# Two attention and two gated-unit layers on one core: tiles three and four as a pair, a shared tail in the output projection, and a last down projection in 288-column pieces

## The chip, the cores and the metric

The kernel runs on one core of a Trainium2 chip. The metric is the device time in microseconds of one execution; lower is better. PE is the matmul engine (TensorE), DVE the vector engine, ACT the scalar engine, POOL is GpSimd, and SP issues the DMAs. All times are in us unless ns is written.

## The reference

The input is 2048 rows of 576 numbers. Four layers follow each other, each with a residual addition: attention, gated unit, attention, gated unit, with the same weights in both rounds.

```python
def _A_ref(x, wqkv, wo):          # H = 32 heads of 18, W = 8 positions, dilation 2
    qkv = (lambda x, *d: x.transpose(*d))((x @ wqkv).reshape(B, S, 3, H, Dh), 2, 0, 3, 1, 4)
...
    idx = pos[:, None] - off[None, :]          # off = 0, 2, ..., 14
    logits = einsum("bhsd,bhswd->bhsw", q, kg) * scale
    attn = softmax(where(mask, logits, -1e9))
    o = einsum("bhsw,bhswd->bhsd", attn, vg)
    return o.reshape(B, S, D) @ wo
def _B_ref(x, w_gate, w_up, w_down):           # F = 4608
    return ((x @ w_gate) * (x @ w_up)) @ w_down
x = x + _A_ref(_layernorm(x), ...)
x = x + _B_ref(_layernorm(x), ...)
x = x + _A_ref(_layernorm(x), ...)
x = x + _B_ref(_layernorm(x), ...)
```

A position attends to itself and the seven positions 2, 4, ..., 14 before it, so an attention tile needs only 14 rows (the halo) of the tile ahead of it.

## The kernel before

**Tiles and items.** The 2048 rows are 16 tiles of 128. They are worked on in items: an item is one tile (`nst` = 1) or a pair of tiles (`nst` = 2) in one attention layer and the gated unit behind it. `seq` (L1042 to L1049) lists them: for the first eight tiles, layer pair 0 and then layer pair 1; then the same for the last eight. The first four tiles are single items in layer pair 0, everything else is in pairs, so there are 18 items, numbered `j` from 0. All weights but w_down stay in SBUF. w_down is read again for each item, in 18 loads of 288 KB (L840 to L848) into seven buffers.

**An item's attention** (`attention`, L493). `head` (L406) makes the layer norm of the tile's rows and their transpose: statistics on DVE (L414, L415), the root on ACT (L429, L430), a small DVE step (L433), the normalised rows on ACT (L439), and the transpose. For `j` < 5 the transpose is made on PE (six instructions, L452 and L454) through the single PSUM bank `pa` and copied out by ACT (L457); later items use a DMA transpose (L445). Then come the QKV projection (`project`, L517; matmuls L527; evacuation by ACT and DVE), the scores on DVE (products L676 or L697, sums L680 to L685), the sum over each head on PE (L691), the softmax on DVE and ACT (L717 to L733), the spread of the weights over the heads' partitions (on PE and ACT, L742 and L748, for `j` < 5; by DMA through DRAM otherwise, L752 and L755), the weighted sum of v on DVE (L772, L786) into `oT`, the output projection on PE (L805 for pairs, L826 for single tiles), the residual addition on DVE (L796), and a second `head`, whose result `xnT_B` feeds the gated unit.

**Half arrays.** For pairs, most matmuls read only 64 of the array's 128 rows. `both` (L464) alternates those on the lower and on the upper 64 rows, which write different PSUM banks, so that two run side by side. Each accumulation is made in two passes, `first` and not; between them a one-element ACT copy (`fence`, L469, L471) keeps the passes apart. Single tiles use the full array (L876, L928), except for the last 64 of the 576 contracted rows (L887).

**The output projection of a pair** (L797 to L819). `oT` has 576 numbers a row in five groups: four of 128 and a last one, `t` = 4, of 64, which stands in partitions 0 to 63. `strip(i, r, hh, first)` lists the matmuls of tile `i`, array half `r` and column half `hh`. The lower half has five of them, the upper four, in each of the four strips, since the last group is only in the lower partitions.

**The gated unit** (`glu`, L853). 36 blocks of 128 columns of gate and up. A pair takes units of two blocks (`quarter`, L894), a single tile units of four blocks in groups of three units (`full`, `tails`, L871 to L892). `evac` (L907): ACT copies the gate (L911), DVE multiplies (L912). The down projection follows in three phases (`down`, L919, for single tiles; `down2`, L957, for pairs), each followed by additions to the residual on DVE (L939, L941 or L948). The pair's down projection writes 512 columns into one PSUM bank and 64 into another. The very last one of the kernel is written out in an order of its own (L991 to L999) on the full array: eight blocks of the second tile, all twelve of the first, the last four of the second; each tile is then added (512 and 64 columns) and stored with one DMA of 144 KB.

**What sets the order.** Nothing is issued directly. Each step is recorded with `op(engine, cost, function, reads, writes, ...)`, and `Plan.run` (L84) lists them: it keeps a clock for each engine from the costs written in the code, and takes again and again the step that can start first, with ranks and margins (`rank`, `prio`, `margin`) that decide between items. The functions are then called in that order, and each engine runs its instructions strictly in it. PSUM banks are handed out by the same plan: `unit` (pairs of banks), `pa` (one bank) and `boot`. At `j` == 4 (L1070) the banks `pa` and `acct` join the units. While PE has nothing to do before the first gated unit, the plan fills it with idle matmuls (L1077).

`xtmp` (L300) is room inside the residual buffer `xf` in which the rows of the fifth and sixth tile are loaded early, so that the fifth item's `head` can run ahead; `guard` (L792) keeps the item that writes there behind its readers. `place` (L484) says which q, k, v buffers an item uses.

Of the kernel before, what the change touches and what calls it, by code (L numbers as in the profile page):

```python
# [169 lines left out]
def kernel(  # L170
# [78 lines left out]
    wd = [sb(f"wd{i}", [P, 2, D]) for i in range(NWD)]  # L249

# [80 lines left out]
    def setup_b():  # L331
        def mk_zero():
            for t_ in qT_:
                nc.gpsimd.memset(t_[TL:P, KF, :], 0.0)
            for t_ in kv_:
                nc.gpsimd.memset(t_[TL:P, :, KF, :], 0.0)
            nc.gpsimd.memset(q_x[TL:P, KF, :], 0.0)
            nc.gpsimd.memset(kv_x[TL:P, :, KF, :], 0.0)
            for t_ in halo:
                nc.gpsimd.memset(t_[:], 0.0)  # L340
            nc.gpsimd.memset(wo_p[TL:P, KF, :], 0.0)
        op("POOL", 2600, mk_zero, w=[f"{x}{t}{i}" for x in "qkv" for t in (4, "H") for i in ZN] + [f"halo{i}" for i in range(n_al)] + ["wo_z"])
# [61 lines left out]
    wok = ["wo_z", "wot0", "wot1"] + [f"wo{dd}" for dd in range(4)]  # L404

    def head(src, keys, nst, dst, key, prio, ab, on_pe, mg, c0=0, halves=False):  # L406
# [3 lines left out]
        for i in range(nst):  # L410
            def stats(i=i):
                xr = src(i).rearrange("p (a b) -> p a b", a=2)
                for a in range(2):
                    nc.vector.bn_stats(out=st[:, ia + i, a, :], in_=xr[:, a, :])  # L414
                nc.vector.bn_aggr(out=mv[:, ia + i, :], in_=st[:, ia + i])  # L415
# [7 lines left out]
            op("DVE", 970, stats, r=[keys[i]], w=[f"mv{ab}{ia + i}", f"st{ab}{ia + i}0", f"st{ab}{ia + i}1"], prio=prio)  # L423
# [4 lines left out]
        def rs():  # L428
# [3 lines left out]
        op("ACT", 440, rs, r=mk + ["eps"], w=rk, prio=prio)  # L432
        op("DVE", 75, lambda: nc.vector.scalar_tensor_tensor(nmr[:, sl], mv[:, sl, 0], -1.0, rstd[:, sl], op0=ALU.mult, op1=ALU.mult),  # L433
           r=mk + rk, w=nk, prio=prio)
        for i in range(nst):
# [6 lines left out]
            op("ACT", 770 if on_pe else 1100, apply, r=[keys[i], nk[i], rk[i]], w=[f"xn{ab}{ia + i}"], prio=prio)  # L442
# [41 lines left out]
    def place(j, nst):  # L484
        if nst == 1:
            z, h = j // 2, j % 2
            return [2 * z + h], qT_[z][:, :, h * P:h * P + P], kv_[z][:, :, :, h * (HALO + P):(h + 1) * (HALO + P)], h * P
        if j == 4:
            return ["x"], q_x, kv_x, 0
        z = (j + 1) % 2  # L490
        return [2 * z, 2 * z + 1], qT_[z][:], kv_[z][:, :, :, 0:HALO + CH], 0

    def attention(j, la, t0, nst):  # L493
# [3 lines left out]
        on_pe = j < 5  # L497
        prio, mg = (1, 0) if fast else (3, 500 if j < 6 else 1200)
# [7 lines left out]
        if j != 4:  # L506
            head(lambda i: xin[:, i0 + i, :], xin_k, nst, xnT_A, "xA", prio, 0, on_pe, mg, c0)
# [9 lines left out]
        def project(tag, au, bu, tl, ea, eb, dkeys):  # L517
# [32 lines left out]
            if nst == 2:  # L550
                o = None
                fs = {ka: {}, kb: {}}
                for first in (True, False):
                    for u, key, parts in ((ua, ka, au), (ub, kb, bu)):
                        r0, r1 = (0, 1) if first else (1, 0)
                        kw = dict(pair=(ua, ub), margin=400) if o is None else dict(after=o, need=u)
# [30 lines left out]
            else:  # L587
# [11 lines left out]
                o1 = pieces(ua, au, ka, True, False, late["wo"] if 2 <= j < 4 else None, margin=400, pair=(ua, ub))  # L599
# [44 lines left out]
        else:  # L644
# [89 lines left out]
        op("DVE", 86 + 2.05 * n, soft3, r=["Lt", "zs"], w=["s13"], prio=prio - 1)  # L734
        if on_pe:
# [56 lines left out]
        guard = {3: ["xt0", "xt1"], 5: zk_x}.get(j, [])  # L792
# [4 lines left out]
        if nst == 2:  # L797
# [4 lines left out]
            def strip(i, r, hh, first):  # L802
                def one(t):
                    rows = slice(TL * r, TL * r + TL)
                    return nc.tensor.matmul(bank(hh, us[i])[:, 0:HD], lhsT=oT[rows, t, i * P:(i + 1) * P], rhs=wo_p[rows, t, hh * HD:(hh + 1) * HD],  # L805
                                     start=(first and t == 0), stop=(not first and t >= KF - 1), skip_group_check=True)
                return [lambda t=t: one(t) for t in range(KF + 1 - r)]
            for first in (True, False):
                for i in range(nst):
                    kw = dict(pair=tuple(us), margin=mg) if o is None else dict(after=o, need=us[i])  # L810
                    o = op("PE", KT * TILE * HD, lambda i=i, first=first: both(strip(i, 0, 0 if first else 1, first), strip(i, 1, 1 if first else 0, first),
                                                                                           None if first else fs[i]),
                           r=["oT", "oTt", *wok], w=[f"wo{j}_{i}"], prio=0, half=True, **kw)
                    if first:
                        fence(fs[i], lambda i=i: bank(0, us[i])[0:1, 0:1], [f"wo{j}_{i}"])
# [17 lines left out]
        head(lambda i: xs_f[:, i0 + i, :], fk, nst, xnT_B[j % NXB], f"xB{j % NXB}_", prio - 1, 1, on_pe, mg, halves=fast)  # L833
# [19 lines left out]
    def glu(j, t0, nst, last):  # L853
# [103 lines left out]
        def down2(ph, hsl, half):  # L957
# [33 lines left out]
            todo = {0: spans(ph), 1: spans(ph)}  # L991
            lead = spans(ph)[:8]
            order = [(1, x) for x in lead] + [(0, x) for x in spans(ph)] + [(1, x) for x in spans(ph)[8:]]
            for x, (i, (m, e, ft)) in enumerate(order):
                kw = dict(pair=(use, tl)) if x == 0 else {}
                bb("PE", 122, lambda i=i, m=m, e=e, ft=ft: [f() for f in two(i, slice(0, P), m, e, ft, ft == n0, ft == n1)],
                   r=[f"h{hsl[m]}", f"wd{wb(ft)}"], w=[f"acc{j}_{ph}{i}"], **kw)
                if ft == n1:
                    settle2(i, use, tl, True, f"acc{j}_{ph}{i}")  # L999

        units = {}
        for ph in range(nph):
# [37 lines left out]
            settle(ph, use)  # L1040

    seq = []  # L1042
# [12 lines left out]
    load_x(2, 1)  # L1055
    load_x(3, 1)
# [6 lines left out]
    for j, (l, t0, nst) in enumerate(seq):  # L1063
        if l == 0 and j >= 4:
            load_x(t0, nst)
# [4 lines left out]
        if j == 4:  # L1070
# [40 lines left out]
```

## Time and profile before

| | us |
|---|---|
| median of 3 runs | 1057.23 (1056.66 to 1058.14) |
| the profiled execution | 1056.22 |
| its span in the profile | 1054.4 |
| granted TensorE clock in it | 0.998 |

The span runs from the first to the last instruction of the profiled execution; 1.8 us of that execution lie outside it. In the profile's rows of groups stand the line, the engine, the operation, what is written and read, the shapes, the count, then the busy time in us and the mean duration of one in ns, and after the second bar the idle time of the engine ahead of them. In the timeline's rows stand the start, the duration, the engine, the line and the same names. Matmuls overlap: their price is the step from one start to the next, not the duration.

### The profile page before, as it was taken

The page shows a single profiled execution, that of the slowest core. Times are in us where ns is not written, and L with a number is a line of the kernel's source. Part 1 is how long each engine was busy: PE and PEld are TensorE (multiplying, and loading weights), DVE is VectorE, ACT ScalarE, POOL GpSimd, SP SyncE. Part 2 cuts the span into 40 slices and gives each one's busy share as a digit, 9 for nine tenths or more (in the row PEclk, how much of TensorE's full clock was granted, in tenths as well). Part 3 has the DMA queues.
Part 4 walks back from the last instruction along what each step waited for, and adds up shares of the span by engine and source line. Part 5 has one row for each costly group of instructions (what it writes and reads, how often), then busy time and mean ns, then how long its engine had stood idle before and what let it go on. Part 6 is the DMA issues. An engine that isn't in the chain of part 4 may idle for free.

```text
span 1054.4 us, 39972 instructions
## 1 busy us (share of the span) xinstructions
PE 1040.7 (99%) x17845; PEld 829.9 (79%) x17863; DVE 786.2 (75%) x1477; ACT 410.8 (39%) x1090; POOL 8.9 (1%) x33
## 2 busy tenths in 40 slices
PE   7999999999999999999999999999999999999998
PEld 4888878787788898778887777877887788777776
DVE  7688989786979996979798876676878758833332
ACT  6752254343334544333434323334344252232221
POOL 3000000000000000000000000000000000000000
PEclk9999999999999999999999999999999999999999
DMA  9966563524262543254444534334353334343332
GB/s 272 317 186 194 177 185 104 155 63 145 69 149 81 146 105 107 70 149 128 120 93 107 140 114 118 93 115 95 93 151 82 99 90 126 116 135 96 116 101 69
DMA packets 146828, 133.68 MB, mean 127 GB/s; under 512 B 42272, under 2 KB 146016, under 8 KB 146656
## 3 DMA queue, kind: packets, MB, share of 16 engines
q1 hardware_dynamic: 146656, 131.13, 44.1%
q8 instruction: 139, 2.28, 0.9%
q14 instruction: 33, 0.27, 0.1%
HBM read 118.51 MB, written 4.06 MB: 116 GB/s over the span
## 4 chain that ended last, share of the span: by engine, by line
PE 82%; DVE 11%; DMA 4%; SPq 1%; issue 1%; ACT 1%; DVEq 0%; ACTq 0%
PE pg L900 15%; PE pu L900 14%; PE pu L968 9%; PE pg L968 8%; PE pa L900 5%; PE acct L900 5%; PE pg L527 4%; PE pu L527 3%; PE pu L876 3%; PE pg L876 3%; PE pg L928 2%; DVE scr L772 2%; DVE oT L786 2%; DMA scr<-a_dram 2%; DVE h L912 2%; PE pg L805 1%
## 5 line engine op out<-in xcount | busy, mean ns | idle before, releaser
L900 PE MATMUL pg<-xnT_B,wg 64*128 64x256 bf16 x3072 | 395.3, 269 | 0.5 <-DVE xf L796 0.5
L900 PE MATMUL pu<-xnT_B,wu 64*128 64x256 bf16 x3072 | 395.0, 269 | 0.5
L900 PEld LDWEIGHTS <-wg 64*128 64x128 bf16 x4032 | 367.7, 94 | 29.7 <-issue 2.6
L900 PEld LDWEIGHTS <-wu 64*128 64x128 bf16 x4032 | 366.8, 94 | 23.5 <-issue 0.6
L968 PE MATMUL pg<-wd,h 64*128 64x512 bf16 (+1 forms) x972 | 252.0, 377 | 0.8 <-DVE h L912 0.8
L968 PE MATMUL pu<-wd,h 64*128 64x512 bf16 (+1 forms) x971 | 252.1, 377 | 0.0
L912 DVE TENSOR_TENSOR h<-pu,g_sb 128x512 bf16<-128x512 f32 x228 | 153.5, 686 | 73.8 <-ACT g_sb L911 69.7
L968 PEld LDWEIGHTS <-h 64*128 64x128 bf16 (+1 forms) x1992 | 115.1, 94 | 100.3 <-DVE h L912 2.9
L911 ACT CAST g_sb<-pg 128x512 bf16<-128x512 f32 x228 | 132.1, 586 | 127.6 <-PE pg L900 91.6
L471 ACT COPY tok<-pu 1x1 f32<-1x1 f32 x254 | 37.4, 147 | 258.7 <-PE pu L900 191.8
L900 PE MATMUL acct<-xnT_B,wg 64*128 64x256 bf16 x960 | 130.7, 269 | 0.0
L900 PE MATMUL pa<-xnT_B,wu 64*128 64x256 bf16 x960 | 130.6, 269 | 0.0
L969 PEld LDWEIGHTS <-h 64*128 64x128 bf16 (+1 forms) x1992 | 114.1, 95 | 1.3 <-issue 0.6
L527 PEld LDWEIGHTS <-wqkv 64*128 64x128 bf16 (+1 forms) x2044 | 103.2, 94 | 15.0 <-issue 2.6
L900 PE MATMUL pg<-xnT_B,wgu_t 64*128 64x256 bf16 x384 | 103.3, 269 | 0.0
L900 PE MATMUL pu<-xnT_B,wgu_t 64*128 64x256 bf16 x384 | 103.3, 269 | 0.0
L969 PE MATMUL pa<-wd,h 64*128 64x64 bf16 (+1 forms) x540 | 102.1, 189 | 0.1
L969 PE MATMUL acct<-wd,h 64*128 64x64 bf16 (+1 forms) x540 | 102.1, 189 | 0.0
L697 DVE TENSOR_TENSOR scr<-qT,kv 128x1280 bf16<-128x1280 bf16 x104 | 82.4, 816 | 25.9 <-ACT kv L611 25.9
L786 DVE TENSOR_TENSOR oT<-oT,scr 128x1280 bf16<-128x1280 bf16 (+1 forms) x119 | 90.9, 764 | 3.2
L527 PE MATMUL pg<-xnT_A,wqkv 64*128 64x256 bf16 (+2 forms) x826 | 92.6, 260 | 0.5 <-ACT wqkv L355 0.3
L527 PE MATMUL pu<-xnT_A,wqkv 64*128 64x256 bf16 (+2 forms) x786 | 90.1, 262 | 0.8 <-DVE kv L609 0.4
(156 smaller groups left out, 1598.2 us busy)
## 6 DMA issues: line engine op xcount, KB each, us to landing
wd<-in_B_w_down_dram SPq DMA_DIRECT2D x324, 288.0 KB, 4.4
scr<-a_dram SPq DMA_DIRECT2D x52, 128.0 KB, 2.7
wg<-in_B_w_gate_dram SPq DMA_DIRECT2D x6, 768.0 KB, 10.0
wu<-in_B_w_up_dram SPq DMA_DIRECT2D x6, 768.0 KB, 11.3
out_dram<-xf SPq DMA_DIRECT2D x16, 144.0 KB, 3.0
xb<-in_A_x_dram SPq DMA_DIRECT2D x6, 288.0 KB, 2.9
a_dram<-scr SPq DMA_DIRECT2D x13, 128.0 KB, 2.4
scr<-in_A_wqkv_dram SPq DMA_DIRECT2D x4, 288.0 KB, 3.6
```

The source lines that it names most:

```text
L471: box["at"] = nc.scalar.copy(tok[0:1, :], src())
L527: return nc.tensor.matmul(bank(p_, u)[0:m, e * n:(e + 1) * n], lhsT=wqkv[r_, k, w0:w0 + m], rhs=xnT_A[r_, k, c0:c0 + n], start=start, stop ...
L697: op("DVE", 70 + 2.6 * n, lambda p_=p_, e=e: nc.vector.tensor_tensor(late["prod"][p_ % 2][:, e, :, 0:n], qT[:, :, 0:n], kT[:, :, HALO - DI ...
L772: nc.vector.tensor_tensor(js(dst), js(vT[:, :, o0:o0 + n]), abw, op=ALU.mult)
L786: op("DVE", 70 + 2.63 * n, lambda i_=i_: nc.vector.tensor_tensor(oT[:, :, 0:n], oT[:, :, 0:n], late["prod"][i_ % 2][:, 0, :, 0:n], op=ALU. ...
L876: nc.tensor.matmul(pt[:, e * n:(e + 1) * n], lhsT=w_[:, k, ft * P:(ft + 1) * P], rhs=xT[:, k, 0:n], start=(first and k == 0 and e == 0), s ...
L900: return nc.tensor.matmul(ps[:, e * n:(e + 1) * n], lhsT=w_, rhs=xT[rows, k, 0:n], start=(first and e == 0 and k == 0), stop=(not first an ...
L911: op("ACT", 490, lambda: nc.scalar.copy(g_sb[gs][:, 0:ul], pg[use["slot"]][:, 0:ul]), r=[f"wg_{j}_{u}"], w=[f"g{gs}"], prio=0, due=True)
L912: op("DVE", 605, lambda: nc.vector.tensor_tensor(hb[hs][:, 0:ul], pu[use["slot"]][:, 0:ul], g_sb[gs][:, 0:ul], op=ALU.mult), r=[f"wu_{j}_{ ...
L928: nc.tensor.matmul((pg, pu)[i][use["slot"]][:], lhsT=lhs, rhs=wt[:, e % 2, 0:512], start=first, stop=fin)
L968: return [lambda: nc.tensor.matmul((pg, pu)[i][use["slot"]][:], lhsT=lhs, rhs=wt[rows, e % 2, 0:512], start=first, stop=fin, skip_group_ch ...
L969: lambda: nc.tensor.matmul((pg, pu)[i][tl["slot"]][:, 0:TL], lhsT=lhs, rhs=wt[rows, e % 2, 512:D], start=first, stop=fin, skip_group_check ...
```

## The change

- `seq`: only the first two tiles are single items; tiles three and four become one pair, the third item (`j` = 2). There are 17 items, and every later item's number falls by one. `on_pe` (transposes and spread on PE) now holds for `j` < 3, `pa` and `acct` join the units at `j` == 2, and the numbers in `place`, `guard` and the margins move with it. The rows of the fifth item (the seventh and eighth tile) also go through `xtmp`: its `head` is cut in two (`parts`), the normalisation being recorded at `j` == 2 behind the softmax and the transpose, by DMA, at `j` == 3. The second `head` of `j` == 2 gets a higher priority, a smaller margin and its statistics in halves.
- Output projection: the last 64 rows of wo are loaded into both partition halves, and ACT copies the second tile's last group of `oT` to partitions 64 to 127. The first tile's last matmul runs on the lower half of the array and the second tile's on the upper.
- The very last down projection: each tile's 576 columns in two pieces of 288, each with its own bank, addition and store of 72 KB; the results go through `outb`, the first x buffer.

```diff
+    outb = xb[0]
...
-            nc.gpsimd.memset(wo_p[TL:P, KF, :], 0.0)
...
         for dd in range(2):
-            op("SP", 470, dma(wo_p[32 * dd:32 * dd + 32, KF, :], wv_[:, 16 + dd, :]), w=[f"wot{dd}"], nbytes=32 * D * 2, prio=2.6)
+            for r_ in (0, TL):
+                op("SP", 470, dma(wo_p[r_ + 32 * dd:r_ + 32 * dd + 32, KF, :], wv_[:, 16 + dd, :]), w=[f"wot{dd}{r_}"], nbytes=32 * D * 2, prio=2.6)
...
-        on_pe = j < 5
-        prio, mg = (1, 0) if fast else (3, 500 if j < 6 else 1200)
+        on_pe = j < 3
+        prio, mg = (1, 0) if fast else (3, 500 if j < 5 else 1200)
...
-        if j != 4:
+        if j not in (3, 4):
             head(lambda i: xin[:, i0 + i, :], xin_k, nst, xnT_A, "xA", prio, 0, on_pe, mg, c0)
...
+        if j == 2:
+            pl.rank = 3
+            head(lambda i: xtmp[:, i, :], ["xt0", "xt1"], NST, xnT_A, "xA", prio, 0, on_pe, mg)
+            pl.rank = 4
+            load_x(6, 2, True)
+            pl.rank = 2
         if j == 3:
             pl.rank = 4
-            head(lambda i: xtmp[:, i, :], ["xt0", "xt1"], NST, xnT_A, "xA", prio, 0, on_pe, mg)
+            head(lambda i: xtmp[:, i, :], ["xt0", "xt1"], NST, xnT_A, "xA", prio, 0, False, mg, parts="t")
             pl.rank = 3
...
+        if j == 2:
+            pl.rank = 4
+            head(lambda i: xtmp[:, i, :], ["xt0", "xt1"], NST, xnT_A, "xA", prio, 0, False, mg, parts="n", xr=["s13"])
+            pl.rank = 2
...
-                return [lambda t=t: one(t) for t in range(KF + 1 - r)]
+                return [lambda t=t: one(t) for t in range(KF + (i == r))]
+            op("ACT", 280, lambda: nc.scalar.copy(oT[TL:P, KF, P:2 * P], oT[0:TL, KF, P:2 * P]), r=["oT"], w=["oTt"], prio=prio)
...
-                    o = op("PE", KT * TILE * HD, lambda i=i, first=first: both(strip(i, 0, 0 if first else 1, first), strip(i, 1, 1 if first else 0, first),
-                                                                                           None if first else fs[i]),
+                    o = op("PE", (KF + 0.5) * TILE * HD, lambda i=i, first=first: both(*[strip(i, r, r if first else 1 - r, first) for r in (i, 1 - i)],
+                                                                                      None if first else fs[i]),
...
-        head(lambda i: xs_f[:, i0 + i, :], fk, nst, xnT_B[j % NXB], f"xB{j % NXB}_", prio - 1, 1, on_pe, mg, halves=fast)
+        head(lambda i: xs_f[:, i0 + i, :], fk, nst, xnT_B[j % NXB], f"xB{j % NXB}_", 0 if j == 2 else prio - 1, 1, on_pe, 200 if j == 2 else mg, halves=fast or j == 2)
...
-            order = [(1, x) for x in lead] + [(0, x) for x in spans(ph)] + [(1, x) for x in spans(ph)[8:]]
+            pts = [(0, 0), (0, 1), (1, 0), (1, 1)]
+            order = [(p_, x) for p_ in pts[:3] for x in lead] + [(p_, x) for p_ in pts[:3] for x in rest] + [(pts[3], x) for x in lead + rest]
...
+                    op("DVE", 370, lambda i=i, u=u, cs=cs, at=at: nc.vector.tensor_tensor(at, (pg, pu)[i][u["slot"]][:, 0:HD], xs_f[:, i0 + i, cs], op=ALU.add),
+                       r=[f"acc{j}_{ph}{i}{hh}", fk[i]], w=[f"ob{i}{hh}"], prio=0, free="unit", use=u)
+                    op("SP", 600, dma(ov[:, t0 + i, cs], at), r=[f"ob{i}{hh}"], nbytes=P * HD * 2, prio=2)
...
-                nst = 1 if l == 0 and t < 4 else NST
+                nst = 1 if l == 0 and t < 2 else NST
...
-    load_x(2, 1)
-    load_x(3, 1)
+    load_x(2, 2)
...
-        if j == 4:
+        if j == 2:
             op("PE", 0, lambda: None, w=list(pool_keys["pa"]) + ["acct"], free="unit", use={"slot": NB})
```

More of the change, by code (lines that the diff above doesn't have):

```diff
@@ L340, in mk_zero @@
                 nc.gpsimd.memset(t_[:], 0.0)
-            nc.gpsimd.memset(wo_p[TL:P, KF, :], 0.0)
-        op("POOL", 2600, mk_zero, w=[f"{x}{t}{i}" for x in "qkv" for t in (4, "H") for i in ZN] + [f"halo{i}" for i in range(n_al)] + ["wo_z"])
+        op("POOL", 2600, mk_zero, w=[f"{x}{t}{i}" for x in "qkv" for t in (4, "H") for i in ZN] + [f"halo{i}" for i in range(n_al)])
         for k in range(KT):
@@ L431, in head @@
         rk = [f"rstd{ab}{ia + i}" for i in range(nst)]
-        op("ACT", 440, rs, r=mk + ["eps"], w=rk, prio=prio)
-        op("DVE", 75, lambda: nc.vector.scalar_tensor_tensor(nmr[:, sl], mv[:, sl, 0], -1.0, rstd[:, sl], op0=ALU.mult, op1=ALU.mult),
-           r=mk + rk, w=nk, prio=prio)
+        if "n" in parts:
+            op("ACT", 440, rs, r=mk + ["eps"], w=rk, prio=prio)
+            op("DVE", 75, lambda: nc.vector.scalar_tensor_tensor(nmr[:, sl], mv[:, sl, 0], -1.0, rstd[:, sl], op0=ALU.mult, op1=ALU.mult),
+               r=mk + rk, w=nk, prio=prio)
         for i in range(nst):
@@ L555, in project @@
                         r0, r1 = (0, 1) if first else (1, 0)
-                        kw = dict(pair=(ua, ub), margin=400) if o is None else dict(after=o, need=u)
+                        kw = dict(pair=(ua, ub), margin=400, after=late.get({2: "wo", 4: "glu1"}.get(j))) if o is None else dict(after=o, need=u)
                         o = op("PE", len(parts) // 2 * (KF + first) * TILE * n, lambda u=u, parts=parts, first=first, r0=r0, r1=r1: both(
@@ L1040, in glu @@
             settle(ph, use)
+        late[f"glu{j}"] = chain["pe"]
     seq = []
```

40 lines of the change are left out of this document (23 added, 17 removed).

## The prediction

> **What bounds the kernel now.** I read the page's engine shares first, then the waits of PE, then its timeline stage by stage.
>
> ```profile
> span 1054.4 us, 39972 instructions
> PE 1040.7 (99%) x17845; PEld 829.9 (79%) x17863; DVE 786.2 (75%) x1477; ACT 410.8 (39%) x1090; POOL 8.9 (1%) x33
> ```
>
> ```profile
> PE acct L1077 <- DVE g_sb L1081: 1.2, 1, 1.2
> ...
> PE acct L1077 <- issue: 0.2, 1, 0.2
> ```
>
> PE is busy 99% of the span. Its table of waits has 14 rows, of which these are the first and the last; all together hold about 9 us, most of it before the first gated unit at 33.6 us. So from 33.6 us on the matmul stream sets the end, and the change is worth what it takes out of that stream, less any new wait in it. DVE at 75% and ACT at 39% matter only where PE has to wait for them.
>
> How PE's time goes, in the timeline: a single tile's gated unit, then a pair's.
>
> ```profile
> 33.10 0.39 PE L452 MATMUL pa<-ident,xn 128*128 128x128 bf16 x4
> ...
> 33.60 1.07 PE L876 MATMUL pg<-xnT_B,wg 128*128 128x128 bf16 x16
> 34.50 1.06 PE L876 MATMUL pu<-xnT_B,wu 128*128 128x128 bf16 x16
> 35.40 1.06 PE L876 MATMUL pg<-xnT_B,wg 128*128 128x128 bf16 x16
> 36.38 0.23 PE L887 MATMUL pg<-xnT_B,wgu_t 64*128 64x128 bf16 x1
> ...
> 37.01 0.22 PE L887 MATMUL pg<-xnT_B,wgu_t 64*128 64x128 bf16 x1
> ...
> 37.16 0.40 PE L452 MATMUL pa<-ident,xn 128*128 128x128 bf16 x4
> ```
>
> ```profile
> 204.00 0.27 PE L900 MATMUL pg<-xnT_B,wg 64*128 64x256 bf16 x1
> 204.11 0.27 PE L900 MATMUL pg<-xnT_B,wg 64*128 64x256 bf16 x1
> ...
> 207.32 0.38 PE L968 MATMUL pu<-wd,h 64*128 64x512 bf16 x1
> ...
> 207.57 0.38 PE L968 MATMUL pu<-wd,h 64*128 64x512 bf16 x1
> ```
>
> Matmuls overlap, so their price is the step from start to start. 16 full 128-column matmuls take 0.90, 0.056 each. The 24 half-array tails (twelve slots of two) take 0.055 a slot. In the pair's form a slot is two half-array matmuls side by side: 0.109 for 256 columns, 0.245 for 512+64. Changing between full and half array costs 0.08 (36.38 instead of 36.30) to 0.10 (37.16 instead of 37.06). One transposition (six instructions) costs 0.50 (33.10 to 33.60).
>
> **Part 1, the pair instead of two single tiles.** By the two kernels' instruction order, out go 576 full 128-column matmuls of L876 (32.2), 144 tails (72 slots, 4.0), 72 steps of the down projection (at the pair's 0.245, 17.6), 112 full and 28 half QKV matmuls (7.0) and 20 full matmuls of the output projection (at the 0.123 of part 2, 2.5): 63.3. In come 324 slots of L900 (35.4), 72 of the down projection (17.6), 63 of QKV at 0.110 (6.9), 18 of the output projection (2.2): 62.1. Net -1.2. Two transpositions fewer (12 become 10, since the fourth item's second normalised block goes by DMA): -1.0. Changes between full and half array fall from 54 to 35: 19 at 0.08, -1.5. 18 loads of down weights disappear; PE never waits for one, so they count nothing.
>
> **Part 2, the output projection's shared tail.**
>
> ```profile
> 165.74 0.29 PE L805 MATMUL pg<-wo_p,oT 64*128 64x288 bf16 x1
> ...
> 166.24 0.28 PE L805 MATMUL pg<-wo_p,oT 64*128 64x288 bf16 x1
> 166.25 0.28 PE L805 MATMUL pu<-wo_p,oT 64*128 64x288 bf16 x1
> 166.37 0.28 PE L805 MATMUL pg<-wo_p,oT 64*128 64x288 bf16 x1
> ...
> 167.84 0.53 PE L805 MATMUL pu<-wo_p,oT 64*128 64x288 bf16 x3
> 168.30 0.39 PE L928 MATMUL pg<-wd,h 128*128 128x512 bf16 x1
> ```
>
> A pair has 36 matmuls here, 20 on the lower half of the array and 16 on the upper. They fill 165.74 to 168.30; less 0.10 for the change of mode that is 2.46, twenty steps of 0.123. The lower half sets it. The change gives each half 18, so two steps, 0.245, go per pair; 14 old pairs: -3.4. The price is one ScalarE copy of 64x128 between the last oT addition and the first of these matmuls. No row has this copy; the casts of 64x128 take 0.26 to 0.27, so 15 copies are 4 us on an engine that is 39% busy. PE has units of an earlier item to run meanwhile, so I count nothing; uncovered it would be about 0.4 with its hand-over, 6 us over 15 pairs.
>
> The Trainium skill (TensorE: Matmul & The Clock Gate, Part 3, The mechanism) says that matmuls start and end strictly in program order. The trace differs: the pu row of 166.25 comes later in the program than the pg row of 166.37, yet starts first, so an idle half does run ahead. By that rule the lost slot could not be used by anything; by the trace it could, which leaves the second rival below its chance.
>
> **Part 3, the tail.**
>
> ```profile
> 1050.23 0.38 PE L968 MATMUL pu<-wd,h 128*128 128x512 bf16 x1
> ...
> 1050.65 0.69 DVE L948 TENSOR_TENSOR xf<-pu,xf 128x512 bf16<-128x512 f32 x1
> ...
> 1051.44 0.23 DVE L948 TENSOR_TENSOR xf<-pa,xf 128x64 bf16<-128x64 f32 x1
> L796 DVE TENSOR_TENSOR xf<-pu,xf 128x288 f32<-128x288 f32 x13 | 5.8, 448 | 0.0
> ```
>
> ```profile
> scr<-in_A_wqkv_dram SPq DMA_DIRECT2D x4, 288.0 KB, 3.6
> scr<-in_A_wqkv_dram SPq DMA_DIRECT2D x6, 144.0 KB, 2.8
> scr<-in_A_wqkv_dram SPq DMA_DIRECT2D x2, 72.0 KB, 3.0
> ```
>
> 48 matmuls of 288 columns at 0.123 replace 24 of 512+64 at 0.245: the same 5.9. After the last, one addition of 0.45 replaces 0.69 and 0.23 (1050.65 to 1051.67): -0.55. The last store halves to 72 KB. If its landing shrank with the bytes it would give another 1 us or more; the rows of 144 and 72 KB (2.8 and 3.0) show no shrinking. I take -0.05 for it, -0.6 for the tail, between -0.4 and -1.6.
>
> The Trainium skill (DMA: Bandwidth & Descriptors, Rules for kernel authors) speaks against this split: it would join many small transfers into one, and calls those under 64 KB mostly overhead. The three rows agree as far as they go; by the rule the tail is the -0.55 of the addition.
>
> **Part 4, the new hand-over.** In the changed order the third item's gated unit starts right behind its own second transposition, with nothing between; before, every transposition but the first item's stood 8 us or more ahead of its use.
>
> ```profile
> 31.69 0.40 PE L452 MATMUL pg<-ident,xn 128*128 128x128 bf16 x4 [0.49 <-ACT xn L439]
> ```
>
> ```profile
> 32.31 0.69 ACT L457 COPY xnT_B<-pg 128x640 bf16<-128x640 bf16 x1 [0.67 <-PE pg L454]
> 171.57 0.29 ACT L429 ACTIVATE rstd<-mv,eps_t 128x2 f32<-128x2 f32 x1 [0.69 <-DVE mv L415]
> 172.39 0.87 ACT L439 ACTIVATE xn<-xf,nmr,rstd 128x576 bf16<-128x576 f32 x1 [0.25 <-DVE nmr L433]
> ```
>
> From the start of a transposition to the end of its copy are 1.3 us, PE's own part 0.5: at least 0.9 of idle PE. It is more if the chain ahead of it is longer than the work beside it. From the end of the output projection: a product in front 0.3, four residual additions at 0.37 and a settling 0.7, statistics 2.0 (four at 0.42, two small ones), two small ACT steps 0.5, two DVE products ahead of the next scalar step 1.5, two normalisations 1.7 with PSUM copies between them 1.0, then the first transposition's copy 0.7, three QKV evacuations 1.4 and the last copy 0.7, less 0.9 where steps overlap: 11.1. PE has beside it eight down-projection matmuls 1.0, all of the fifth item's QKV 6.9, two transpositions 1.0, mode changes 0.3: 9.2. I take +1.9 (bounds 0.9 and, with the lateness below, 6).
>
> **Part 5, is DVE in time for the pair?** Two whole single units (27 us each with the attention between) now cover a pair's attention, and two more items' preparation.
>
> ```profile
> L912 DVE TENSOR_TENSOR h<-pu,g_sb 128x512 bf16<-128x512 f32 x228 | 153.5, 686 | 73.8 <-ACT g_sb L911 69.7 <-PE pu L876 2.8
> L697 DVE TENSOR_TENSOR scr<-qT,kv 128x1280 bf16<-128x1280 bf16 x104 | 82.4, 816 | 25.9 <-ACT kv L611 25.9
> L786 DVE TENSOR_TENSOR oT<-oT,scr 128x1280 bf16<-128x1280 bf16 x98 | 80.6, 823 | 2.5
> L680 DVE TENSOR_TENSOR scr<-scr 128x1024 bf16<-128x1024 bf16 x56 | 38.6, 689 | 1.5
> L414 DVE BATCH_NORM_STATS2 st<-xf 128x6 f32<-128x288 f32 x94 | 37.6, 442 | 0.0
> ```
>
> ```profile
> 34.00:61.00 27.00, 26.95 (x477) 23.81 (x477) 20.14 (x45) 16.36 (x37) 0.00 (x0) 1.00 1.08 313
> 61.00:108.00 47.00, 46.79 (x735) 37.67 (x734) 38.62 (x91) 18.79 (x41) 0.00 (x0) 1.00 0.53 164
> 108.00:160.00 52.00, 51.58 (x790) 41.06 (x794) 46.54 (x95) 21.97 (x48) 0.00 (x0) 1.00 0.63 184
> ```
>
> By its order, from the second tile's first product (34.5) to the pair's last oT addition, DVE has (steps of adjoining instructions, some 0.04 to 0.08 under the durations above): 17 products g*u at 0.60 (10.3), five settlings (3.6), the single's attention (15.8) and residual (1.8), the pair's (8 products 6.2, sums 6.0, softmax 3.6, 15 multiplies and adds 11.7: 27.5) and statistics for two later items (3.1): 62.1. PE reaches the pair's output projection at 33.6 + 70.5 of stream + 3.7 of mode changes = 107.8. DVE must be busy 62.1 / 73.3 = 85%. In the windows of before (fourth number: DVE busy) it was busy 79% between 34 and 108, with less to do, and 90% between 108 and 160, with a pair on it. Walking through its known idle places (6 us in the single's softmax, 3 to 4 in the pair's) I come out about 1 us in time. I add 0.3 for small waits here and behind.
>
> What is left: two more small loads of wo ahead of the gate weights and one x load fewer delay those by 0.5 us, against a first use some 10 us after landing; the missing POOL memset and the earlier release of the last PSUM pair count nothing.
>
> **Sum**, against the profiled execution's 1056.22 (span 1054.4 and 1.8 around it): -1.2 - 1.0 - 1.5 - 3.4 - 0.6 + 1.9 + 0.3 = -5.5, so 1050.7. The median of the three runs, 1057.23, is 1.0 above that execution: **1051.7**.
>
> **Rivals.**
> - *The hand-over is free*: normalisation ends earlier and only the 0.9 of the last copy, or not even that, remains. -7.1: about 1050. For it: before, PE lost almost nothing after 33.6. Against: nothing stands between transposition and use.
> - *The odd matmul was no loss*: the half that runs ahead is filled by the next half-array work, or the copy and the fences eat the gain. +3.4: 1055.1. Against: the twenty steps above, up to a following full-array matmul.
> - *DVE somewhat late*: at 82% busy, as between 61 and 108 before, it ends 2.5 us after PE wants it: 1053.5 to 1056.
> - *DVE late, slower than before*: PE stands at the pair's output projection until the oT additions end. At 75% busy, the share of 34 to 61 before, DVE ends 9.5 us late: 1061. It turns slower than before below 77%. For it: the single's softmax alone idles 6 us. Against: 90% with a pair before.
>
> **How the numbers follow.** Forecast 0.53 (own range 1050 to 1053.5), free hand-over 0.13, no gain from the tail 0.09, somewhat late 0.16, late 0.09. About 0.2%, 2.1 us, is what a measurement of this kernel can tell from no change: the bounds are 1055.1 and 1059.3. Faster: 0.53 + 0.13 + half of 0.09 + most of 0.16 = 0.80; same 0.12; slower 0.08. The range runs from the free hand-over with a better tail, 1049.2, to the late end of the third rival, 1056.4.
>
> **What would show it.** L805 should take 18 steps of 0.123 a pair. A wait of 1 to 3 us of L900 on the ACT copy near 120 us should be the only new one; waits of L805 on ACT or DVE near 108 would be the last two rivals; DVE's last addition should be 0.45. Waits of PE spread over all the pairs, or a later first gated unit than 33.6, would make the sum wrong.

## The result, and the profile after

The changed kernel takes 1055.59 us (median of 22 runs, 1053.70 to 1058.59) beside 1057.71 for the kernel before (22 runs, 1055.81 to 1058.78): ratio 0.9983, 95% interval 0.9976 to 0.9990. That is -2.1 us by the medians, where -5.5 was forecast. The profiled execution, at 1053.80 one of the shorter ones, is 2.4 below the profiled one of before.

Page of the changed kernel: span, and busy time of the engines.

```profile
span 1051.9 us, 39994 instructions
...
PE 1032.0 (98%) x17891; PEld 824.9 (78%) x17901; DVE 782.6 (74%) x1443; ACT 414.1 (39%) x1120; POOL 8.0 (1%) x32
```

PE is busy 8.7 us less than before (1040.7), but the span is only 2.5 shorter: 6.2 us of the gain became idle time of PE. The waits of PE say on whom it waits (line waited for, us in total, times, longest). In the changed kernel:

```profile
PE pg L916 <- DVE xf L811: 2.0, 2, 1.4
PE pu L916 <- DVE h L928: 1.7, 2, 0.9
...
PE pa L985 <- DVE h L928: 1.1, 1, 1.1
...
PE pg L916 <- ACT xnT_B L462: 1.1, 1, 1.1
PE pu L985 <- DVE h L928: 1.1, 1, 1.1
...
PE pa L916 <- DVE h L928: 1.0, 1, 1.0
...
PE acct L916 <- DVE xf L811: 0.7, 1, 0.7
```

The same waits in the kernel before, where L796 and L912 are these lines:

```profile
PE pg L968 <- DVE h L912: 0.8, 3, 0.4
...
PE pg L900 <- DVE xf L796: 0.5, 1, 0.5
...
PE pu L969 <- DVE xf L796: 0.2, 1, 0.2
```

All rows together grow from 8.2 us (14 rows; the prediction put them at about 9) to 16.0 (19 rows). Waits for DVE's residual additions (L811) and g*u products (L928) grow from 1.5 to 7.6; one for ScalarE's copy at the hand-over of the third item adds 1.1. All of the DVE waits lie behind 150 us: 0.8 at 157 us in the gated unit of the new pair itself, 2.8 between 260 and 315 us in that of the fifth item and at its end, and 4.0 behind 420 us in items that the change only renumbers.

**One of them, followed.** First PE, then DVE in the changed kernel's timeline:

```profile
514.70 0.28 PE L820 MATMUL pg<-wo_p,oT 64*128 64x288 bf16 x1
516.67 0.27 PE L916 MATMUL pg<-xnT_B,wg 64*128 64x256 bf16 x1 [1.45 <-DVE xf L811]
```

```profile
512.32 1.55 DVE L708 TENSOR_TENSOR scr<-qT,kv 128x1280 bf16<-128x1280 bf16 x2
513.90 0.69 DVE L691 TENSOR_TENSOR scr<-scr 128x1024 bf16<-128x1024 bf16 x1
514.63 0.42 DVE L695 TENSOR_TENSOR scr<-scr 128x512 bf16<-128x512 bf16 x1
515.09 0.42 DVE L696 TENSOR_TENSOR scr<-scr 128x512 bf16<-128x512 bf16 x1
515.43 0.82 DVE L708 TENSOR_TENSOR scr<-qT,kv 128x1280 bf16<-128x1280 bf16 x1
516.17 0.45 DVE L811 TENSOR_TENSOR xf<-pg,xb 128x288 f32<-128x288 f32 x1
516.53 0.45 DVE L811 TENSOR_TENSOR xf<-pu,xb 128x288 f32<-128x288 f32 x1
```

The output projection's last matmul starts at 514.70. PE's next unit needs the two banks that the residual additions read. DVE has no gap above 0.04, but it works in its fixed order through the next item's sums and products, and comes to the additions at 516.17; PE stands for 1.45 us.

**Why DVE is late.** Three steps of the changed kernel's DVE, the second and third of which read the result of the one ahead, and four of which none does:

```profile
420.73 0.82 DVE L708 TENSOR_TENSOR scr<-qT,kv 128x1280 bf16<-128x1280 bf16 x1
421.58 0.69 DVE L691 TENSOR_TENSOR scr<-scr 128x1024 bf16<-128x1024 bf16 x1
422.31 0.42 DVE L695 TENSOR_TENSOR scr<-scr 128x512 bf16<-128x512 bf16 x1
```

```profile
464.40 0.82 DVE L708 TENSOR_TENSOR scr<-qT,kv 128x1280 bf16<-128x1280 bf16 x1
465.14 0.68 DVE L928 TENSOR_TENSOR h<-pu,g_sb 128x512 bf16<-128x512 f32 x1
465.74 0.68 DVE L691 TENSOR_TENSOR scr<-scr 128x1024 bf16<-128x1024 bf16 x1
466.33 0.45 DVE L811 TENSOR_TENSOR xf<-acct,xb 128x288 f32<-128x288 f32 x1
```

A product takes 0.74 to the next step when that step is independent (464.40 to 465.14) and 0.85 when it reads the product (420.73 to 421.58); a sum 0.59 and 0.73. Over the whole trace the medians are 0.85 against 0.735 for the product and 0.73 against 0.60 to 0.61 for the sum. The kernel before has the same dependent steps, here one product and its sums:

```profile
176.86 0.81 DVE L697 TENSOR_TENSOR scr<-qT,kv 128x1280 bf16<-128x1280 bf16 x1
177.71 0.69 DVE L680 TENSOR_TENSOR scr<-scr 128x1024 bf16<-128x1024 bf16 x1
178.44 0.42 DVE L684 TENSOR_TENSOR scr<-scr 128x512 bf16<-128x512 bf16 x1
```

The plan's costs, 70 + 2.6 n and 82 + 2.02 n in the code, are 735 and 599 ns for a pair (n = 256): those of the independent case. So wherever the list puts dependent DVE steps behind each other, DVE falls 0.12 us a step behind what the list assumes.

The Trainium skill (Perfetto Trace Analysis, Optimizing Scalar/DVE Operations) gives a DVE step on SBUF an access overhead of about 60 ns and says that the recorded latency shows about twice that, since the half that acknowledges the write overlaps with the next instruction. The independent steps here agree in kind (0.82 recorded, 0.74 to the next, so 0.08 overlap); the dependent ones show that the overlap is lost, with 0.03 on top (0.85).

### The profile page after: what moved, and what is told of

It reads as the page before. It is cut to its first block, busy times and chain, and to the rows that moved or that the text cites. A ratio compares the mean times of both kernels' runs of the same rounds, so it can differ in the third digit from the quotient of the medians.

```text
span 1051.9 us, 39994 instructions
## 1 busy us (share of the span) xinstructions
PE 1032.0 (98%) x17891; PEld 824.9 (78%) x17901; DVE 782.6 (74%) x1443; ACT 414.1 (39%) x1120; POOL 8.0 (1%) x32
## 4 chain that ended last, share of the span: by engine, by line
PE 80%; DVE 14%; DMA 3%; SPq 1%; issue 1%; ACT 1%; DVEq 0%; ACTq 0%
PE pg L916 18%; PE pu L916 16%; PE pg L984 8%; PE pu L984 8%; PE acct L916 5%; PE pa L916 5%; PE pg L532 3%; DVE oT L801 3%; DVE scr L787 2%; PE pu L532 2%; DVE scr L708 2%; PE acct L984 2%; DVE h L928 2%; PE pa L984 2%; PE pu L892 1%; PE pg L944 1%
## 5 line engine op out<-in xcount | busy, mean ns | idle before, releaser
L916 PE MATMUL pg<-xnT_B,wg 64*128 64x256 bf16 x3296 | 427.4, 269 | 3.1 <-DVE xf L811 2.0
L916 PE MATMUL pu<-xnT_B,wu 64*128 64x256 bf16 x3296 | 425.7, 269 | 1.9 <-DVE h L928 1.7
L916 PEld LDWEIGHTS <-wg 64*128 64x128 bf16 x4320 | 398.3, 94 | 32.6 <-issue 4.7
L916 PEld LDWEIGHTS <-wu 64*128 64x128 bf16 x4320 | 399.5, 94 | 26.0 <-issue 4.1
L984 PE MATMUL pu<-wd,h 64*128 64x512 bf16 x864 | 223.3, 377 | 0.1
L984 PE MATMUL pg<-wd,h 64*128 64x512 bf16 x864 | 223.4, 377 | 0.0
L984 PEld LDWEIGHTS <-h 64*128 64x128 bf16 x2112 | 114.8, 94 | 106.6 <-issue 3.0
L928 DVE TENSOR_TENSOR h<-pu,g_sb 128x512 bf16<-128x512 f32 x224 | 152.3, 687 | 51.1 <-ACT g_sb L927 49.1
L985 PEld LDWEIGHTS <-h 64*128 64x128 bf16 x2112 | 115.8, 95 | 1.2 <-issue 0.3
L985 PE MATMUL pu<-wd,h 64*128 64x64 bf16 x600 | 113.4, 189 | 1.1 <-DVE h L928 1.1
L985 PE MATMUL pg<-wd,h 64*128 64x64 bf16 x600 | 113.4, 189 | 0.0
L532 PE MATMUL pu<-xnT_A,wqkv 64*128 64x256 bf16 (+1 forms) x843 | 98.9, 266 | 1.2 <-ACT wqkv L355 0.9
```

The lines of the kernel that those rows point to most:

```text
L532: return nc.tensor.matmul(bank(p_, u)[0:m, e * n:(e + 1) * n], lhsT=wqkv[r_, k, w0:w0 + m], rhs=xnT_A[r_, k, c0:c0 + n], start=start, stop ...
L916: return nc.tensor.matmul(ps[:, e * n:(e + 1) * n], lhsT=w_, rhs=xT[rows, k, 0:n], start=(first and e == 0 and k == 0), stop=(not first an ...
L928: op("DVE", 605, lambda: nc.vector.tensor_tensor(hb[hs][:, 0:ul], pu[use["slot"]][:, 0:ul], g_sb[gs][:, 0:ul], op=ALU.mult), r=[f"wu_{j}_{ ...
L984: return [lambda: nc.tensor.matmul((pg, pu)[i][use["slot"]][:], lhsT=lhs, rhs=wt[rows, e % 2, 0:512], start=first, stop=fin, skip_group_ch ...
L985: lambda: nc.tensor.matmul((pg, pu)[i][tl["slot"]][:, 0:TL], lhsT=lhs, rhs=wt[rows, e % 2, 512:D], start=first, stop=fin, skip_group_check ...
```

## The experiments

Two theories. **A, the order:** PE's new waits come from a DVE that is later than the list assumes, in an order in which the releases of PSUM banks have too little room; the shorter output projection takes some of that room away. **B, the pair:** the new waits come with tiles three and four as a pair and the items that move with it. Further rivals stand in the expectations. Each ratio is against the kernel before on the same chip, with its 95% interval.

**tail_alone** is the kernel before with only the shared tail of the output projection:

```diff
+            for r_ in (0, TL):
+                op("SP", 470, dma(wo_p[r_ + 32 * dd:r_ + 32 * dd + 32, KF, :], wv_[:, 16 + dd, :]), w=[f"wot{dd}{r_}"], nbytes=32 * D * 2, prio=2.6)
...
-                return [lambda t=t: one(t) for t in range(KF + 1 - r)]
+                return [lambda t=t: one(t) for t in range(KF + (i == r))]
+            op("ACT", 280, lambda: nc.scalar.copy(oT[TL:P, KF, P:2 * P], oT[0:TL, KF, P:2 * P]), r=["oT"], w=["oTt"], prio=prio)
...
-                    o = op("PE", KT * TILE * HD, lambda i=i, first=first: both(strip(i, 0, 0 if first else 1, first), strip(i, 1, 1 if first else 0, first),
-                                                                                           None if first else fs[i]),
+                    o = op("PE", (KF + 0.5) * TILE * HD, lambda i=i, first=first: both(*[strip(i, r, r if first else 1 - r, first) for r in (i, 1 - i)],
+                                                                                      None if first else fs[i]),
...
```

> The kernel before with only the shared tail of the output projection (wo's last rows in both halves, the ScalarE copy, 18 instead of 20 steps a pair). In the changed kernel PE waited 16.0 us by its rows of waits, 8.2 before; 7.6 of the 16.0 end with DVE's residual additions (L811) or g*u products (L928), 1.5 before. Theory A, the order: the list of steps is made with costs in which a DVE step that reads the result of the step just before it costs no more than another; the trace shows 0.12 more (0.85 against 0.73 for a product behind a product's sum, 0.73 against 0.61 for a sum). So DVE runs 2 us later against PE than listed, and wherever the list leaves a PSUM bank's release less room, PE waits; the shorter projection takes room away and reorders the additions. Walking through this order with the trace's steps gives 3.4 us less stream and about 5 us more waits: 1059 to 1060 (before 1057.7). Rival B, the waits come with the pair of tiles three and four: none of them here, 1054.3.

Measured: 1058.47 us beside 1057.39, ratio 1.0013 (1.0004 to 1.0021). Alone, the part that was to save most makes the kernel slightly slower. In its waits of PE:

```profile
PE pg L901 <- DVE xf L796: 2.2, 3, 1.0
...
PE pu L970 <- DVE h L913: 1.2, 1, 1.2
PE pu L901 <- DVE h L913: 1.2, 1, 1.2
```

There is no pair of tiles three and four here, and the same waits are there: all rows of these two DVE steps sum to 7.0 us, where the kernel before has 1.5. B falls.

**without_tail** is the changed kernel with the projection as before:

```diff
-                return [lambda t=t: one(t) for t in range(KF + (i == r))]
-            op("ACT", 280, lambda: nc.scalar.copy(oT[TL:P, KF, P:2 * P], oT[0:TL, KF, P:2 * P]), r=["oT"], w=["oTt"], prio=prio)
+                return [lambda t=t: one(t) for t in range(KF + 1 - r)]
...
-                    o = op("PE", (KF + 0.5) * TILE * HD, lambda i=i, first=first: both(*[strip(i, r, r if first else 1 - r, first) for r in (i, 1 - i)],
+                    o = op("PE", KT * TILE * HD, lambda i=i, first=first: both(strip(i, 0, 0 if first else 1, first), strip(i, 1, 1 if first else 0, first),
...
```

> The changed kernel with the output projection as before (20 steps a pair, no ScalarE copy). Theory A: 3.4 us more stream, some 5 to 6 us fewer waits behind DVE: 1053 to 1054, faster than the changed kernel's 1055.6; the waits near 264, 467, 516 and 803 us shrink from 0.7 to 1.6 to 0.5 or less. Rival B, the waits come with the pair: they stay, 1059.0.

Measured: 1052.45 us beside 1057.39, ratio 0.9952 (0.9938 to 0.9965). It beats the whole change by 3 us, though its stream is longer by two steps in each of 15 pairs (3.7 us). All rows of the two DVE steps sum to 2.8 us instead of 7.6; the largest:

```profile
PE acct L983 <- DVE h L927: 0.6, 1, 0.6
PE pa L983 <- DVE h L927: 0.6, 1, 0.6
```

**after_dve_cost** and **before_dve_cost** change no instruction. In either kernel the plan alone is told that a DVE step which depends on the step just before it starts 118 ns later. This holds behind steps with a cost above 400 ns, other than those with costs of 600, 605 and 970 (additions to the residual, g*u products, statistics):

```diff
+        o.raw = eng == "DVE" and cost > 400 and cost not in (600, 605, 970)
...
                 t = max(t, clock[o.eng])
+                if o.eng == "DVE" and self.last is not None and self.last in o.deps and self.last.raw:
+                    t = max(t, clock["DVE"] + 118)
...
             clock[o.eng] = o.end
+            if o.eng == "DVE":
+                self.last = o
```

> The changed kernel with the same instructions, listed in an order that reckons 0.118 us more for a DVE step that reads the result of the step just before it. Theory A: the 6 us of waits behind DVE after 150 us fall to 2 or 3, and lists that fit close up elsewhere too: 1046 to 1049. Rival C, the waits come from the copy's hand-over or from transfers and not from the order: 1055 to 1056.

> The kernel before, same instructions, with the same 0.118 us in the making of its order. Theory A: before loses to the same error, though less: its waits after 33 us fall from some 4 to 6 us to 1 to 2: 1051 to 1054. If the error costs only the changed kernel anything, 1057.7. The difference to the run before it is then what the change is worth under a fitting order: by the prediction's terms without waits 5 to 7 us.

Measured: 1047.55 us for the changed kernel in its new order (ratio 0.9903, 0.9890 to 0.9915) and 1052.62 for the kernel before in its own (0.9954, 0.9942 to 0.9966), both beside 1057.39. The order alone is worth 8 us to the one and 5 to the other. The largest waits of the reordered changed kernel for these two DVE steps:

```profile
PE pg L990 <- DVE h L934: 1.3, 2, 0.7
...
PE pu L991 <- DVE h L934: 0.5, 1, 0.5
PE pg L922 <- DVE xf L817: 0.4, 1, 0.4
```

7.6 us of waits for DVE have become 2.2. In the kernel before under its new order, this is the only row that is left of the two steps:

```profile
PE pg L974 <- DVE h L918: 0.2, 1, 0.2
```

But there the rows hold little of the gain: all together go from 8.2 to 7.7 us, while the span falls by 4.4 (1054.4 to 1050.0) and PE's busy time by 3.3 (1040.7 to 1037.4) with the same instructions. A row counts a wait from the modelled end of the last matmul. A pair's matmul of 256 columns is recorded 0.27 long, but the next starts 0.109 later, so about the first 0.16 of a stall is counted as busy. Counted from start to start instead (what a step takes beyond the usual one for its shape, where that is more than 0.06), PE loses about 7 us behind the start of the first gated unit in the kernel before, 13 in the changed one, and 4 and 8 in the two new orders. So fewer stalls make about 3 of the 4.4 us in the one and 5 to 6 of the 6.5 in the other; the rest isn't traced to a wait.

One row of the windows, 160 to 580 us, shows the stage in which they lay (length; busy PE, PEld, DVE, ACT, POOL, each with its count; clock; DMA share; GB/s). Before, changed, tail_alone, and the changed kernel reordered:

```profile
160.00:580.00 420.00, 417.70 (x7306) 339.87 (x7308) 360.58 (x650) 171.48 (x475) 0.00 (x0) 1.00 0.42 112
```

```profile
160.00:580.00 420.00, 413.43 (x7322) 342.22 (x7320) 365.69 (x667) 172.80 (x482) 0.00 (x0) 1.00 0.42 112
```

```profile
160.00:580.00 420.00, 413.01 (x7247) 346.50 (x7249) 357.34 (x645) 171.05 (x475) 0.00 (x0) 1.00 0.42 112
```

```profile
160.00:580.00 420.00, 418.98 (x7443) 342.79 (x7444) 344.54 (x641) 171.16 (x479) 0.00 (x0) 1.00 0.44 117
```

PE is idle for 2.3, 6.6, 7.0 and 1.0 us of these 420. DVE's busy time falls from 366 to 345 though the program is the same: with other steps between dependent ones part of the penalty is gone, and part of its work has moved elsewhere (over the whole span it falls from 782.6 to 771.2).

**notail_dve_cost** puts the two edits together: the changed kernel without the shared tail, listed with the 118 ns.

> The changed kernel with the output projection as before (20 steps a pair, no ScalarE copy), listed with the 0.118 us for dependent DVE steps. Beside the run of the same list with the shared tail (1047.6) it gives the tail's worth under a fitting order. If the two steps saved a pair are all won once the order fits: 3.4 us longer, 1051. If part of them is lost since DVE, near 90% busy in the first half, sets the time there: walking through the order with the trace's steps gives 1 us longer, 1048.6.

Measured: 1049.59 us beside 1057.71, ratio 0.9923 (0.9910 to 0.9937). Against 0.9903 with the tail, the tail is worth 0.20%, 2.1 us, in a fitting order. With the two intervals that is uncertain by some 1.9, so the run doesn't tell the 1 us of the walk through the order from the 3.4 (3.7 with the new pair's two steps) that PE's stream gets shorter; it does show that the tail is no longer a loss.

**tail_old_list** has the instructions of tail_alone, listed with the old projection's cost and none for the copy:

```diff
-            op("ACT", 280, lambda: nc.scalar.copy(oT[TL:P, KF, P:2 * P], oT[0:TL, KF, P:2 * P]), r=["oT"], w=["oTt"], prio=prio)
+            op("ACT", 0, lambda: nc.scalar.copy(oT[TL:P, KF, P:2 * P], oT[0:TL, KF, P:2 * P]), r=["oT"], w=["oTt"], prio=prio)
...
-                    o = op("PE", (KF + 0.5) * TILE * HD, lambda i=i, first=first: both(*[strip(i, r, r if first else 1 - r, first) for r in (i, 1 - i)],
+                    o = op("PE", KT * TILE * HD, lambda i=i, first=first: both(*[strip(i, r, r if first else 1 - r, first) for r in (i, 1 - i)],
```

> The instructions of the run with the shared tail alone, but listed as if the projection still took 20 steps and the ScalarE copy nothing, so that DVE's order differs from that of before at 42 instead of 289 of 1281 listed steps. With the tail alone and its own list the kernel was 1.1 us slower than before, though the tail takes 3.4 us out of PE's stream: 4.5 us went into waits. If the new order made them: 1054.3 here. If DVE has no room to release the banks two steps earlier, whatever the order: 1058.5. Walking through this order with the trace's steps gives 3.4 us less stream and 2.6 more waits: 1057.

Measured: 1056.01 us beside 1056.78, ratio 0.9990 (0.9981 to 0.9999): -0.8, between the two ends. The rows of the two DVE steps sum to 4.0 us, between the 1.5 of before and the 7.0 of tail_alone. So of the 4.5 us that ate the tail's 3.4 and 1.1 more, about 1.9 (from +1.1 to -0.8) came with the new order and 2.6 from DVE not being ready two steps earlier in nearly the old one. The split is rough: each of the two ratios is uncertain by 0.9 us.

**last_alone** is the kernel before with only the last down projection in 288-column pieces (the change's own diff of that part).

> The kernel before with only the last down projection in 288-column pieces, each stored when done. By the prediction's term -0.6 (bounds -0.4 to -1.6): about 1056.8 beside 1057.4, the order ahead of it being the same. If two stores of 72 KB a tile cost more than one of 144 KB: 1057.4 or later, with the end further behind the last addition than the 2.7 us of before.

Measured: 1056.72 us beside 1057.71, ratio 0.9988 (0.9980 to 0.9997), -1.0 by the medians; the interval, -0.3 to -2.1, holds the -0.6 as well. Its end stands 2.4 behind the last addition, so the two stores cost no more than the one.

**handover_plain** is the changed kernel without the three edits to the third item's second normalisation:

```diff
-        head(lambda i: xs_f[:, i0 + i, :], fk, nst, xnT_B[j % NXB], f"xB{j % NXB}_", 0 if j == 2 else prio - 1, 1, on_pe, 200 if j == 2 else mg, halves=fast or j == 2)
+        head(lambda i: xs_f[:, i0 + i, :], fk, nst, xnT_B[j % NXB], f"xB{j % NXB}_", prio - 1, 1, on_pe, mg, halves=fast)
```

> The changed kernel without the higher priority, smaller margin and halved statistics of the third item's second normalisation. The hand-over of the third item cost 1.3 us of PE time in the changed kernel (a wait of 1.1). If the chain behind the output projection is what PE waits for, the three edits shorten it, and without them PE idles 3 to 5 us before 125 us: 1057 to 1058. If the chain had slack, the time and the waits stay: 1055.6.

Measured: 1058.31 us beside 1057.71, ratio 1.0008 (0.9999 to 1.0017), 2.7 above the changed kernel. PE at the hand-over, in its timeline:

```profile
123.50 0.40 PE L457 MATMUL pa<-ident,xn 128*128 128x128 bf16 x4 [2.19 <-ACT xn L441]
124.81 0.24 PE L702 MATMUL pg<-scr,Esel 128*32 128x128 bf16 x4 [0.46 <-DVE scr L696]
```

PE now waits 2.2 for the normalised rows ahead of the transposition. The chain does set the time there, and the three edits had shortened it. The rest of the 2.7 isn't shown by this alone, since the list behind it differs too: the rows of the two DVE steps sum to 8.5 us here, 7.6 in the changed kernel.

**fitted** is after_dve_cost with two more numbers of the plan changed, together:

```diff
-    LAT = {"PE": 250, "ACT": 150, "DVE": 150, "POOL": 150, "SP": 0}
+    LAT = {"PE": 250, "ACT": 150, "DVE": 200, "POOL": 150, "SP": 0}
...
-        prio, mg = (1, 0) if fast else (3, 500 if j < 5 else 1200)
+        prio, mg = (1, 0) if fast else (3, 500 if j < 5 else 800)
```

> The changed kernel with the same instructions, in a list that reckons 0.118 us for dependent DVE steps, 0.20 instead of 0.15 us from a DVE step to its reader, and a margin of 800 instead of 1200 ns for the later items. Theory A: another 1.5 to 2.5 us of waits go: 1045 to 1046. If the remaining waits don't hang on the order: 1047.6, as with the dependent steps alone.

Measured: 1045.80 us beside 1057.71, ratio 0.9885 (0.9869 to 0.9900). It beats both kernels, by 12 and 10 us, with the changed kernel's instructions and only their order altered (but for six more idle matmuls ahead of the first gated unit). What each of the two numbers is worth wasn't tried apart.

## Why the prediction was wrong, step by step

- **The pair (part 1) and its stream.** Held, as far as the runs can tell. PE's busy time fell by 8.7, where the stream's terms sum to 7.1 (1.2 + 1.0 + 1.5 + 3.4). The 1.6 between them is no finding: the ends of matmuls are modelled, and last_alone, with a stream as long as that of before, shows 1042.9 for 1040.7, and 18 matmuls of before have no record (17845 beside 17863 weight loads). The changes between full and half array fall from 50 to 32 in the two timelines if the short matmuls of L691 are left out, 18 fewer for the 19 of the forecast (74 to 62 with them). Under fitting orders the whole change is worth 0.9903 / 0.9954, 5.4 us with some 1.9 of uncertainty, beside the 5.5 forecast. That the two are so close is in part luck: without the tail it is 0.9923 / 0.9954, 3.3 us, where the other terms sum to 2.1, and the tail adds 2.1 for 3.4.
- **The tail (part 2).** The steps went as forecast: 18 of 0.123. The changed kernel's projection at its first pair:

```profile
108.53 0.29 PE L820 MATMUL pg<-wo_p,oT 64*128 64x288 bf16 x1
...
109.52 0.28 PE L820 MATMUL pu<-wo_p,oT 64*128 64x288 bf16 x1
109.73 0.39 PE L944 MATMUL pg<-wd,h 128*128 128x512 bf16 x1
```

  Nine steps from 108.53 to 109.52 and its end, twice a pair. No wait of L820 is among PE's rows, so the copy was covered, as I had counted; at the first pair it ended 0.9 ahead of the projection:

```profile
107.32 0.30 ACT L823 COPY oT<-oT 64x128 bf16<-64x128 bf16 x1 [0.69 <-DVE oT L801]
```

  What failed is that I took 3.4 us out of the stream and left the engine that has to follow where it was.
- **The kernel's end (part 3).** The changed kernel's last addition, beside 0.69 and 0.23 before:

```profile
1048.97 0.46 DVE L1021 TENSOR_TENSOR xb<-pu,xf 128x288 bf16<-128x288 f32 x1 [1.01 <-PE pu L1014]
```

  From the start of the last additions to their end are 0.46 instead of 1.02 (1050.65 to 1051.67), and from there to the end of the span 2.47 instead of 2.73: -0.8 together, where -0.6 was forecast and last_alone measured -1.0. The Trainium skill (DMA: Bandwidth & Descriptors, Rules for kernel authors) would join many small transfers into a large one and calls those under 64 KB mostly overhead; both stores here are larger. As the prediction read the rule, only the addition was to be won (0.56). The store gave 0.26 more between these two traces, so for 144 against 72 KB they speak against that reading.
- **The hand-over (part 4).** The mechanism was right, the size a little high: PE's gated unit waited 1.1 for the copy where +1.9 was counted.

```profile
120.50 0.40 PE L457 MATMUL pa<-ident,xn 128*128 128x128 bf16 x4
121.45 0.69 ACT L462 COPY xnT_B<-pa 128x640 bf16<-128x640 bf16 x1
122.19 0.27 PE L916 MATMUL pg<-xnT_B,wg 64*128 64x256 bf16 x1 [1.12 <-ACT xnT_B L462]
```

  From the last step of the projection (111.2) to this gated unit are 11.0, where the chain was put at 11.1; PE had 9.9 of work beside it where 9.2 was counted. The "8 us or more" of the prediction holds for second transpositions alone: the first ones stood 2 to 7 us ahead of their use.
- **DVE for the first pair (part 5).** Held: PE reached the projection at 108.53 and did not wait. That is 0.7 later than the 107.8 of the forecast, 0.35 of it since the first gated unit began at 33.95 instead of 33.6. DVE's busy time in the stretch, third of the busy times:

```profile
34.50:107.80 73.30, 72.75 (x1163) 59.14 (x1167) 62.31 (x122) 35.46 (x80) 0.00 (x0) 1.00 0.74 224
```

  The hand sum was 62.1.
- **The step that failed** stands at the end of part 5: "I add 0.3 for small waits here and behind." Behind, the waits for DVE grew by 6.1, which is more than the whole tail was to save. The prediction had named the sign of it itself: waits of PE spread over all the pairs. I had walked through DVE's order for one pair, and for the items after it had taken over from the profile of before that PE hardly waits. But there DVE was busy 86% of 160 to 580 us, and its releases came just in time for the old stream. The rows to see it were in the trace of before: the dependent steps at 176.86 and 177.71 us, 0.12 longer than the costs in the code.
- **The rivals.** "The odd matmul was no loss" came out near the measured time (1055.1), but not by its mechanism: the matmuls were saved, and tail_alone and tail_old_list show the saving going into waits for DVE. "DVE somewhat late" named the engine, but for the one pair at 108 us, where it was in time.

That another order of the same instructions wins back what the change lost is shown by after_dve_cost. That it does so because the 0.12 us is now counted is likely but not shown apart: all three lists that were made with it came out faster than those without (changed, before, without tail, by 8, 5 and 3 us), but no list with an arbitrary other change was run beside them. Nor is it shown that the 0.12 us is the whole of DVE's lateness. Not settled is why single executions of the changed kernel spread over 4.9 us, against 3.0 before: the profile is of a short one, and none of a long one was taken.

## What to carry to other kernels

Before a matmul stream is shortened, look at how late the engine that frees its PSUM banks already is: here that engine was 86% busy and worked in a fixed order, and the saved steps came back as waits for it, items away from the edit. Where a list made from costs sets the order, lay its costs beside the trace first, for dependent and independent neighbours apart: one corrected number was worth 5 to 8 us here, the edits to the instructions 2 to 5. And look for stalls from start to start, since the rows of waits leave out the first part of each. Last, judge an edit under an order that fits it; under the wrong one a good part can measure as a loss.

## What the runs showed of the hardware

- A DVE step on SBUF operands costs about 0.12 us more when it reads what the step just before it wrote (0.85 against 0.74 for 128x1280, 0.73 against 0.60 to 0.61 for 128x1024, bf16). An independent step put between the two hides it (464.40 to 465.74 us above).
- The end of the kernel behind the last addition was 2.73 us with a store of 144 KB and 2.47 with one of 72 KB; over all traces it is 2.6 to 2.8 in the four with 144 KB and 2.4 to 2.6 in the seven with 72.
- The rows of waits understate a stall of PE: a matmul of 256 columns is recorded 0.27 us long where the next starts 0.109 later.
